# The key-value products of a chunk, made one chunk ahead in the scan's two PSUM banks

## The chip, the cores and the metric

The kernel runs on one core of one Trainium2 chip. Its engines each take their instructions in a fixed order: TensorE (PE; its weight loads, PEld, overlap the matmuls), VectorE (DVE), ScalarE (ACT), GpSimd (POOL), and SyncE (SP), which issues the DMAs. The metric is the device time of one execution in microseconds (us), the median of several runs.

## The reference, cut to what matters

Inputs are q, k, v and a complex decay for 4 batches, 8 heads, 768 time steps and 48 features. In float32:

```python
# a_re, a_im: decay, scaled to a magnitude of at most 0.999
for t in range(768):                               # state S: 48 x 48, complex
    S_re, S_im = ar*S_re - ai*S_im + k[t] v[t]^T,  ar*S_im + ai*S_re
    y[t] = q[t] @ S_re
# x = y, heads side by side: (4, 768, 384)
u  = x + real(fft(fft(x, over time), over features))
un = (u - mean) / sqrt(var + 1e-6)                 # over the 384 features
u  = u + relu(un @ w_ch1) @ w_ch2                  # 384 -> 1536 -> 384
u  = u + (relu(u^T @ w_tok1) @ w_tok2)^T           # tokens: 768 -> 256 -> 768
out = u + relu(u @ w_ch1b) @ w_ch2b                # 384 -> 1536 -> 384
```

## The kernel before

The work of a batch is a chain and a dense part. **The chain** (`chain`) begins with `stage1`: a scan along time over the decays, which uses the two PSUM banks of tag "p", then a test that sets a gate (`st_g2`), then the recurrence in 8 chunks of 96 time steps. Behind it comes `stage2`, in which the Fourier sums are made on VectorE (L988, L994, L1005) and TensorE (L1028, L1039, L1044, L1086), and the normalization (L1091 to L1120; ScalarE's last step is L1118). `transposed` (L899 to L911) then turns the normalized tiles: TensorE L906, ScalarE L909 (th, the high part), VectorE L910 (tl, the low part). **The dense part** is `mlp` (TensorE L926 and L948; VectorE adds into u at L951), `tok1` (L1153) and `tok2` (L1171; VectorE L1173). Every fp32 matrix product there is three products of high and low parts. `mlp` takes three token tiles of 128 at once in L926, so it begins when the third of them has its th and tl.

While the chain of batch b+1 runs, the dense part of batch b fills TensorE (in the driver: `chain(b + 1)`, then `dense1(b)` and `mlp2`). The order on each engine is fixed when the program is built, by a scheduler that takes the ready instruction of the best priority: on TensorE the chain goes ahead of the dense work, on the other engines the dense work ahead of the chain (`RANK`, L60). In batch 0 there is no dense work to fill in; there the weights are converted to high and low parts (L185 to L207: VectorE L194 and L199, GpSimd L196 and L206, ScalarE L191 and L205), and stored. Later batches load the converted weights (L283).

**A chunk c.** `ch_load` (L739) issues from SP the DMA of V (L741, tag "P", 2 buffers) and two of Kn, the scaled keys (L744, tag "A", 2 buffers). `ch_sc` (L748) makes the scores, TensorE L753, masked by VectorE (L760). `ch_u` (L763) makes the key-value products (L768 and L769, 8 heads, 16 matmuls), and the state's step from them: VectorE adds the products to the state T (Aa, L779) and multiplies by the decay (Xx, L785), VectorE or GpSimd makes the crossed part (yc, L786 and L787), VectorE adds to the new T (L789). `ch_y` (L794) makes the outputs, scores times V (L802) and state times queries (L808), which ScalarE copies out to xT (L810).

PSUM has eight banks: three of tag "s" (scores, and in batches 1 to 3 key-value products and outputs too: `PU`), three of tag "l" (dense work, and in batch 0 key-value products and outputs), two of "p". Tiles of a tag take its banks in turn, and a matmul into a bank waits for the last reader of what was there.

Of the kernel before, what the change touches and what calls it, by code (L numbers as in the profile page):

```python
# [53 lines left out]
def attn_fft_mixer_kernel(ctx: ExitStack, tc: tile.TileContext, aL, xL, vL, wL, qN, kN, vN, arN, aiN,  # L54
# [37 lines left out]
    def alloc(tag, shape, dt=F32, name=None):  # L92
        n = 1
        for x in shape[1:]:
            n *= x
        t = pool.tile([128, SIZE[tag]], dt, tag=tag, bufs=BUFS[tag], name=name or tag)
        return shaped(t[0:shape[0], 0:n], shape)
# [3 lines left out]
    def palloc(tag, shape):  # L101
        n = 1
        for s in shape[1:]:
            n *= s
        t = psum.tile([128, 512], F32, tag=tag, bufs=PSB[tag], name=tag)
        v = t[0:shape[0], 0:n]
        if len(shape) == 3:
            v = v.rearrange("p (a b) -> p a b", b=shape[2])
        return v
# [195 lines left out]
    def warm(n, x):  # L305

        ps = palloc("l", [128, 512])
        for _ in range(n):
            te.matmul(out=ps[:, 0:x.shape[1]], lhsT=ident[0:x.shape[0], :], rhs=x)
# [391 lines left out]
    def stage1(b):  # L701
# [34 lines left out]
        st = {}  # L736
        PU = "l" if b == 0 else "s"

        def ch_load(c):  # L739
            v = alloc("P", [96, 384], name="V")  # L740
            sp.dma_start(out=v, in_=vL[b, c])  # L741
            kt = alloc("A", [96, 8, 128], name="Kn")
            for hf in range(2):
                sp.dma_start(out=kt[48 * hf:48 * hf + 48],  # L744
                             in_=knd[hf].rearrange("(h c) s f -> c s h f", c=8)[c])
            st[c] = dict(v=v, kt=kt)

        def ch_sc(c, half):  # L748
            ps = palloc("s", [96, 4, 96])
            Q, K = qk[0][:, 1], qk[0][:, 0]  # L750
            for j in range(4):
                hc = (half * 4 + j) * 8 + c
                te.matmul(out=ps[:, j, :], lhsT=K[:, hc, :], rhs=Q[:, hc, :])  # L753
            sc = alloc("e", [96, 4, 96], name="sc")
            mb = mask.unsqueeze(1).to_broadcast([96, 4, 96])
            if half and OFF[2] & (1 << b):
                se.copy(out=sc, in_=ps)
                ge.tensor_tensor(out=sc, in0=sc, in1=mb, op=ALU.mult)
            else:
                ve.tensor_tensor(out=sc, in0=ps, in1=mb, op=ALU.mult)  # L760
            st[c][f"sc{half}"] = sc

        def ch_u(c):  # L763
            d = st[c]
            ps = palloc(PU, [112, 8, 48])
            for h in range(8):
                vv = d["v"][:, h * 48:h * 48 + 48]
                te.matmul(out=ps[0:64, h, :], lhsT=d["kt"][:, h, 0:64], rhs=vv)  # L768
                te.matmul(out=ps[64:112, h, :], lhsT=d["kt"][:, h, 64:112], rhs=vv)  # L769
            g = gm[b % 2].rearrange("p k (h c) -> p k h c", c=8)[:, :, :, c:c + 1]  # L770

            def gb(k, lo, hi):
                return g[lo:hi, k].to_broadcast([hi - lo, 8, 48])

            def v8(ap):
                return ap.rearrange("p (h e) -> p h e", e=48)
            if c:
                a = alloc("e", [112, 384], name="Aa")
                ve.tensor_tensor(out=v8(a), in0=v8(st["T"]), in1=ps, op=ALU.add)  # L779
                a = v8(a)  # L780
            else:
                a = ps
            y = yc[c % 2]
            x = alloc("e", [112, 384], name="Xx")
            ve.tensor_tensor(out=v8(x), in0=a, in1=gb(0, 0, 112), op=ALU.mult)  # L785
            (ge if c and b else ve).tensor_tensor(out=v8(y)[0:48], in0=a[64:112], in1=gb(1, 64, 112), op=ALU.mult)  # L786
            st["yop"] = (ge if c else ve).tensor_tensor(out=v8(y)[64:112], in0=a[0:48], in1=gb(1, 0, 48), op=ALU.mult)  # L787
            T = alloc("e", [112, 384], name="T")
            st["op"] = ve.tensor_tensor(out=T, in0=x, in1=y, op=ALU.add)  # L789
            st["Tn"] = T  # L790
            if b == 0:
                tops.append(st["op"])
# [23 lines left out]
        ch_load(1)  # L816
        ch_sc(0, 0)
        ch_sc(0, 1)
        for c in range(8):
            if c < 7:  # L820
                ch_u(c)
                ch_sc(c + 1, 0)
                ch_sc(c + 1, 1)
            ch_y(c)
            if b == 0 and WC[c]:
                warm(WC[c], ident)
            st["T"] = st.get("Tn")
            if c < 6:
                ch_load(c + 2)
            if b == 0 and c < 7:  # L830
                rests[0], rests[1] = tops[c], st["yop"]
                tick(CF[c + 1], c == 5)
# [368 lines left out]
    def on(s, f, *args):  # L1201
        stream[0] = s
        return f(*args)

    def chain(b):
        stage1(b)
        return stage2(b)
# [3 lines left out]
    u, norm = on(FIRST, chain, 0)  # L1211
    t1 = on(FIRST, transposed, u, norm, "s")
    feed(56)
    for b in range(B - 2):
# [8 lines left out]
        u = u1  # L1223
# [12 lines left out]
    with tc.If(fv != 0):  # L1236
        with tc.For_i(0, B, 1) as b:
            fallback(b)
            u, norm = stage2(B)
# [113 lines left out]
```

## Time and profile before

| | us |
|---|---|
| median of 3 runs | 1102.06 (1101.85 to 1102.67) |
| profiled execution, span of the trace | 1097.6 |
| what lies outside the span (median less span) | 4.5 |
| TensorE busy in the span | 981.1 (89%) |
| VectorE busy | 776.3 (71%) |
| ScalarE busy | 511.7 (47%) |
| GpSimd busy | 420.9 (38%) |

The profiled execution is known by its span; the times of the runs hold a start and an end besides. The chunks of the four batches stand at about 84 to 143, 350 to 405, 545 to 584 and 732 to 782 us of the span. In the rows, an operation has the tile that it writes, "<-", the tiles that it reads, and "x" the number of such instructions in the row. A matmul of fp32 data has two records in the trace for one in the program's order. In square brackets stands how long the engine was idle before, and whose instruction ended that. "SPq" is the queue of DMA issues.

### The profile page before, as it was taken

To read this page: it belongs to the slowest core of one execution; us is meant where nothing else is said; L and a number is where in the kernel's file an instruction comes from. 1 tells how busy PE (TensorE), PEld (TensorE's weight loads), DVE (VectorE), ACT (ScalarE), POOL (GpSimd) and SP (SyncE) were. 2 spreads that over 40 slices of the span, in tenths; PEclk is the share of its full clock that TensorE was granted. 3 is DMA by queue.
4 is the path that set the end of the run, shared out by engine and by line. 5 is a ranking of instruction groups with operands and counts; after the bars stand their busy time and mean duration, and the time that the engine had idled before them with its cause. 6 is when DMAs were issued, how large, how long until landed. Compare 5 with 4: busy or idle time off the path is not lost.

```text
span 1097.6 us, 21079 instructions
## 1 busy us (share of the span) xinstructions
PE 981.1 (89%) x7314; PEld 919.2 (84%) x7314; DVE 776.3 (71%) x2083; ACT 511.7 (47%) x1425; POOL 420.9 (38%) x552
## 2 busy tenths in 40 slices
PE   1358797999889989799998999999897999999997
PEld 0227675989889887799997899999786999999997
DVE  6986987999999668999758879984744433433332
ACT  6753355777877225968315556842234212121111
POOL 6643985573576454345336312424512002000000
PEclk9997797999999999799999999999998999999999
DMA  6136954686758663356664346664303433443432
GB/s 217 45 82 180 298 175 152 220 272 196 233 182 274 201 185 124 110 165 180 158 192 147 107 138 194 186 184 131 122 29 115 144 116 130 159 154 127 165 101 75
DMA packets 101537, 174.66 MB, mean 159 GB/s; under 512 B 11056, under 2 KB 61104, under 8 KB 100912
## 3 DMA queue, kind: packets, MB, share of 16 engines
q1 hardware_dynamic: 101424, 173.24, 51.1%
q8 instruction: 60, 0.98, 0.4%
q14 instruction: 53, 0.43, 0.1%
HBM read 133.88 MB, written 39.32 MB: 158 GB/s over the span
## 4 chain that ended last, share of the span: by engine, by line
PE 64%; DVE 10%; ACT 2%; DMA 2%; issue 1%; POOL 1%; SPq 0%; POOLq 0%; DVEq 0%; ACTq 0%
PE l L948 23%; PE l L926 21%; PE s L753 3%; PE s L642 2%; PE s L1039 2%; PE s L802 2%; DVE ws L994 2%; PE s L1028 1%; PE s L808 1%; PE s L1153 1%; PE s L768 1%; DVE ws L988 1%; PE s L1171 1%; DVE cvt L199 1%; PE s L906 1%
## 5 line engine op out<-in xcount | busy, mean ns | idle before, releaser
L948 PE MATMUL l<-w,h 128*128 128x384 f32 x1728 | 326.8, 340 | 5.7 <-DVE h L939 5.1
L926 PE MATMUL l<-th,w 128*128 128x384 f32 x1152 | 317.2, 344 | 8.8 <-DVE u L951 5.0
L948 PEld LDWEIGHTS l<-w,h 128*128 128x128 f32 x1728 | 298.4, 189 | 10.0 <-DVE h L939 7.2
L926 PEld LDWEIGHTS l<-th,w 128*128 128x128 f32 x1152 | 212.9, 191 | 13.3 <-DVE u L951 6.3
L926 PE MATMUL l<-tl,w 128*128 128x384 f32 x576 | 196.0, 340 | 3.6 <-DVE tl L910 3.6
L930 ACT ACTIVATE h<-l 128x384 fp32r<-128x384 f32 x192 | 94.0, 490 | 212.7 <-PE l L926 212.0
L951 DVE TENSOR_TENSOR u<-u,l 128x384 f32<-128x384 f32 x192 | 105.3, 549 | 81.9 <-PE l L948 80.9
L939 DVE SCALAR_TENSOR_TENSOR h<-l,h 128x384 fp32r<-128x384 f32 x160 | 88.4, 553 | 88.5 <-ACT h L930 88.3
L926 PEld LDWEIGHTS l<-tl,w 128*128 128x128 f32 x576 | 110.1, 191 | 4.1 <-DVE tl L910 4.1
L196 POOL TENSOR_TENSOR cvt<-cvt 128x384 int32<-128x384 int32 x56 | 64.7, 1160 | 36.7 <-DVE cvt L194 11.0
L466 PE MATMUL s<-misc,y 128*112 128x128 f32 x96 | 21.7, 369 | 53.1 <-DVE y L444 48.8
L466 PEld LDWEIGHTS s<-misc,y 128*112 128x112 f32 x96 | 14.0, 177 | 62.3 <-issue 26.8
L753 PE MATMUL s<-qkt 112*96 112x96 f32 x512 | 59.2, 266 | 6.7 <-DVE sc L760 6.7
L753 PEld LDWEIGHTS s<-qkt 112*96 112x96 f32 x512 | 53.2, 177 | 9.4 <-DVE sc L760 7.4
L1138 POOL TENSOR_TENSOR xl<-u,xh 128x384 fp32r<-128x384 f32 x18 | 17.9, 1006 | 105.6 <-ACT xh L1137 105.6
L206 POOL TENSOR_TENSOR w<-cvt,w 128x384 fp32r<-128x384 f32 x44 | 51.2, 1172 | 9.9 <-ACT w L205 6.1
L199 DVE SCALAR_TENSOR_TENSOR cvt<-cvt 128x384 int32<-128x384 int32 x56 | 48.1, 865 | 7.0 <-POOL cvt L196 6.8
L571 POOL TENSOR_TENSOR tm<-tm 128x144 f32<-128x144 f32 (+1 forms) x51 | 27.1, 531 | 59.0 <-ACT tm L570 58.7
L937 POOL TENSOR_TENSOR h<-full,h 128x384 fp32r<-128x384 f32 x32 | 33.6, 1049 | 35.5 <-ACT full L936 33.7
L642 PE MATMUL s<-misc,y 128*112 128x128 f32 x288 | 45.0, 276 | 1.4 <-DVE y L626 1.0
L615 DVE TENSOR_TENSOR p<-p,A 128x144 f32<-128x144 f32 x144 | 44.6, 310 | 2.2
L786 POOL TENSOR_TENSOR yc<-Aa,gm 48x384 f32<-48x384 f32 x18 | 21.0, 1164 | 63.3 <-DVE Aa L779 63.3
(234 smaller groups left out, 1950.8 us busy)
## 6 DMA issues: line engine op xcount, KB each, us to landing
w<-wscr SPq DMA_DIRECT2D x180, 384.0 KB, 3.5
cvt<-wL SPq DMA_DIRECT2D x56, 384.0 KB, 4.6
wscr<-w SPq DMA_DIRECT2D x44, 384.0 KB, 3.5
Kn<-kn SPq DMA_DIRECT2D x64, 192.0 KB, 3.7
kn<-y SPq DMA_DIRECT2D x96, 96.0 KB, 2.5
raw<-aL SPq DMA_DIRECT2D x48, 144.0 KB, 3.2
xx<-xL SPq DMA_DIRECT2D x48, 144.0 KB, 3.1
V<-vL SPq DMA_DIRECT2D x32, 144.0 KB, 3.1
```

What stands on the lines that cost most here:

```text
L196: x = ge.tensor_tensor(out=a, in0=a, in1=lo, op=ALU.add)
L199: rest(ve.scalar_tensor_tensor(out=a, in0=hi, scalar=-0x80000000, in1=a, op0=ALU.bitwise_and, op1=ALU.bitwise_or))
L206: ge.tensor_tensor(out=parts[:, 1, :], in0=a.bitcast(F32), in1=r32(parts[:, 0, :]), op=ALU.subtract)
L466: te.transpose(ps[:, j, :], y[:, j, 0:112], ident)
L615: ve.tensor_tensor(out=cur, in0=prev, in1=A[:, j, 0:3, :], op=ALU.mult)
L642: te.transpose(ps[:, j, :], y[:, j, 0:112], ident)
L753: te.matmul(out=ps[:, j, :], lhsT=K[:, hc, :], rhs=Q[:, hc, :])
L926: te.matmul(out=ps, lhsT=w1[:, wi, kt * 128:kt * 128 + 128], rhs=x[g][:, kt, :], start=(n == 0), stop=(n == 8))
L930: x = se.activation(out=hi, in_=ps, func=ACTF.Relu)
L939: ve.scalar_tensor_tensor(out=lo, in0=ps, scalar=0.0, in1=r32(hi), op0=ALU.max, op1=ALU.subtract)
L948: te.matmul(out=ps, lhsT=hs[m][:, hi, tt * 128:tt * 128 + 128], rhs=w2[:, wi, :], start=(n == 0), stop=(n == 8))
L951: ve.tensor_tensor(out=u[tt], in0=u[tt], in1=ps, op=ALU.add)
```

## The change

`ch_u` is split. `ch_m(c)` makes the 16 key-value products, and into a "p" bank; `ch_u(c)` only reads them. `ch_m(0)` is called before the loop, `ch_m(c + 1)` at the start of step c for c below 6. The scores and outputs stay on their banks.

```diff
-        def ch_u(c):
+        def ch_m(c):
+
             d = st[c]
-            ps = palloc(PU, [112, 8, 48])
+            ps = d["u"] = palloc("p", [112, 8, 48])
             for h in range(8):
                 vv = d["v"][:, h * 48:h * 48 + 48]
                 te.matmul(out=ps[0:64, h, :], lhsT=d["kt"][:, h, 0:64], rhs=vv)
                 te.matmul(out=ps[64:112, h, :], lhsT=d["kt"][:, h, 64:112], rhs=vv)
+
+        def ch_u(c):
+            ps = st[c]["u"]
...
         ch_sc(0, 1)
+        ch_m(0)
         for c in range(8):
             if c < 7:
+                if c < 6:
+                    ch_m(c + 1)
                 ch_u(c)
                 ch_sc(c + 1, 0)
                 ch_sc(c + 1, 1)
```

In the changed kernel the lines shift: the key-value products are L769 and L770, the outputs L806 and L812, and lines behind the chunk loop are 7 higher (L906 becomes L913, L926 L933, L948 L955, L988 L995, L1028 L1035, L1171 L1178, L1173 L1180). The order of the dense work around the chain moves with them.

The first place is TensorE in the chunks of batch 1. L768 and L769 (L769 and L770 after) are the key-value products, L753 the scores, L948 (L955) dense work, L802 and L808 (L806 and L812) the outputs. Before:

```order
686 L768 MATMUL s<-V,Kn 64x48
687 L769 MATMUL s<-V,Kn 48x48
688 L753 MATMUL s<-qkt 96x96 x8
689 L948 MATMUL l<-w,h 128x384 x11
690 L802 MATMUL s<-sc,V 64x96
691 L802 MATMUL s<-sc,V 48x96
692 L808 MATMUL s<-qkt,T 64x96
693 L808 MATMUL s<-qkt,T 48x96
```

After:

```order
718 L955 MATMUL l<-w,h 128x384 x11
719 L806 MATMUL s<-sc,V 64x96
720 L806 MATMUL s<-sc,V 48x96
721 L812 MATMUL s<-qkt,T 64x96
722 L812 MATMUL s<-qkt,T 48x96
723 L806 MATMUL s<-sc,V 64x96
724 L769 MATMUL p<-V,Kn 64x48
725 L770 MATMUL p<-V,Kn 48x48
...
740 L806 MATMUL s<-sc,V 48x96
741 L812 MATMUL s<-qkt,T 64x96
...
750 L812 MATMUL s<-qkt,T 48x96
751 L753 MATMUL s<-qkt 96x96 x8
```

The key-value products, before between the outputs of one chunk and the scores of the next, stand inside the outputs, and write "p" instead of "s".

The second place is TensorE behind the last outputs of batch 2's chunks. L1178 is the second token-mixing product (L1171 before), L906 (L913) the transposes of the tiles u of the dense work, L926 (L933) the first dense product behind them, L1028 (L1035) the first product of the mixing. Before:

```order
1427 L808 MATMUL s<-qkt,T 48x96
1428 L906 MATMUL l<-misc,u_3218 128x128 x3
1429 L926 MATMUL l<-th,w 128x384
1430 L926 MATMUL l<-tl,w 128x384
...
1453 L926 MATMUL l<-th,w 128x384
1454 L1028 MATMUL s<-dcos,ws 128x97 x5
```

After:

```order
1402 L812 MATMUL s<-qkt,T 48x96
1403 L1178 MATMUL l<-R,w 128x384 x19
1404 L913 MATMUL l<-misc,u_3213 128x128 x3
1405 L913 MATMUL l<-misc,u_3214 128x128 x3
1406 L913 MATMUL l<-misc,u_3215 128x128 x3
1407 L913 MATMUL l<-misc,u_3216 128x128 x3
1408 L1035 MATMUL s<-dcos,ws 128x97 x3
1409 L913 MATMUL l<-misc,u_3217 128x128 x3
1410 L1035 MATMUL s<-dcos,ws 128x97 x9
1411 L913 MATMUL l<-misc,u_3218 128x128 x3
1412 L933 MATMUL l<-th,w 128x384
```

Before, dense products (36 in all, in pieces of one or two) stood between the last transposes and the first mixing products; after, the end of the token mixing and six groups of transposes stand there, and dense products begin behind the second piece of the mixing.

On VectorE at the same place, L1173 (L1180) adds the token mixing into u, L910 (L917) makes tl, and L988, L994 and L1005 (L995, L1001 and L1012) are the first steps of the mixing. Before:

```order
1297 L760 TENSOR_TENSOR sc<-s,misc 96x384 x2
1298 L910 TENSOR_TENSOR tl<-l,th 128x3x128 x3
1299 L988 TENSOR_TENSOR ws<-xT 112x4x288
1300 L988 TENSOR_TENSOR ws<-xT 112x4x96
1301 L994 TENSOR_TENSOR ws<-ws 112x2x288
1302 L910 TENSOR_TENSOR tl<-l,th 128x3x128
1303 L994 TENSOR_TENSOR ws<-ws 112x2x288
1304 L994 TENSOR_TENSOR ws<-ws 112x2x96 x2
...
1306 L994 TENSOR_TENSOR ws<-ws 112x2x288
1307 L1005 TENSOR_TENSOR ws<-ws 112x2x191 x2
```

After:

```order
1292 L995 TENSOR_TENSOR ws<-xT 112x4x288
1293 L1180 TENSOR_TENSOR u_3215<-u_3215,l 128x384
1294 L995 TENSOR_TENSOR ws<-xT 112x4x96
1295 L1180 TENSOR_TENSOR u_3216<-u_3216,l 128x384
1296 L1001 TENSOR_TENSOR ws<-ws 112x2x288 x2
1297 L1180 TENSOR_TENSOR u_3217<-u_3217,l 128x384
1298 L1001 TENSOR_TENSOR ws<-ws 112x2x96 x2
...
1300 L1180 TENSOR_TENSOR u_3218<-u_3218,l 128x384
1301 L917 TENSOR_TENSOR tl<-l,th 128x3x128
1302 L1001 TENSOR_TENSOR ws<-ws 112x2x96
1303 L1012 TENSOR_TENSOR ws<-ws 112x2x191 x4
...
1308 L917 TENSOR_TENSOR tl<-l,th 128x3x128
```

The tl of the first token tiles, before made ahead of or inside the mixing's first steps, stand behind most of them.

The third place is TensorE at the end of batch 3's chain, where L906 (L913) turns the normalized tiles and L1153 (L1160) is the first token-mixing product of batch 2. Before:

```order
2096 L1086 MATMUL s<-misc,xT 128x112 x4
2097 L1086 MATMUL s<-misc,ws 128x112 x4
2098 L948 MATMUL l<-w,h 128x384 x9
2099 L906 MATMUL s<-misc,ws 128x128 x18
2100 L1153 MATMUL s<-xh,w 128x384 x10
```

After:

```order
2072 L955 MATMUL l<-w,h 128x384 x6
2073 L913 MATMUL s<-misc,ws 128x128 x6
2074 L955 MATMUL l<-w,h 128x384 x2
2075 L913 MATMUL s<-misc,ws 128x128 x3
2076 L955 MATMUL l<-w,h 128x384 x19
2077 L913 MATMUL s<-misc,ws 128x128 x3
2078 L955 MATMUL l<-w,h 128x384 x8
2079 L913 MATMUL s<-misc,ws 128x128 x3
2080 L955 MATMUL l<-w,h 128x384 x19
2081 L1160 MATMUL s<-xh,w 128x384 x5
```

The 18 transposes stood together behind the last dense products that were left; after, dense products stand among and behind them.

## Rows read from the trace of the kernel before

**Rows 1.** Stretches: window, length, busy PE, PEld, DVE, ACT, POOL, clock, DMA, GB/s

```profile
84.00:143.00 59.00, 47.69 (x640) 44.12 (x636) 47.49 (x86) 20.74 (x45) 40.94 (x31) 0.77 0.84 252
...
350.00:405.00 55.00, 53.56 (x724) 50.31 (x723) 35.48 (x79) 16.27 (x36) 22.72 (x22) 1.00 0.71 196
405.00:450.00 45.00, 34.56 (x200) 28.20 (x199) 40.29 (x123) 26.75 (x84) 21.99 (x32) 0.84 0.40 128
...
545.00:584.00 39.00, 39.00 (x603) 35.95 (x602) 22.46 (x44) 7.87 (x16) 12.44 (x13) 1.00 0.62 179
584.00:600.00 16.00, 11.43 (x60) 10.78 (x58) 16.00 (x21) 8.43 (x27) 13.26 (x11) 0.89 0.56 170
...
782.00:837.00 55.00, 44.51 (x266) 38.96 (x264) 33.72 (x69) 20.37 (x55) 23.54 (x22) 0.92 0.25 84
```

**Rows 2.** TensorE's timeline, a chunk and dense work: start, us, operation, idle before

```profile
372.38 0.34 PE L808 MATMUL s<-qkt,T 112*48 112x96 f32 x4
...
373.57 0.92 PE L753 MATMUL s<-qkt 112*96 112x96 f32 x8
...
377.09 0.38 PE L802 MATMUL s<-sc,V 96*64 96x96 f32 x4
...
378.30 0.34 PE L808 MATMUL s<-qkt,T 112*48 112x96 f32 x4
...
463.69 6.50 PE L948 MATMUL l<-w,h 128*128 128x384 f32 x36
```

**Rows 3.** VectorE by line: busy, mean ns, idle before and its releaser

```profile
L779 DVE TENSOR_TENSOR Aa<-T,s 112x384 f32<-112x384 f32 x18 | 10.0, 554 | 24.6 <-PE s L769 24.6
```

**Rows 4.** Weight loads by line

```profile
L802 PEld LDWEIGHTS s<-sc,V 96*48 96x48 f32 (+1 forms) x384 | 20.4, 129 | 5.3 <-DVE T L789 3.0 <-issue 2.3
```

**Rows 5.** SP's timeline in the same chunk of batch 1

```profile
372.60 0.33 SPq L741 DMA_DIRECT2D V<-vL  x1
373.69 1.07 SPq L744 DMA_DIRECT2D Kn<-kn  x2
```

**Rows 6.** Landing of V (L741), batch 1, 355 to 400

```profile
DMA to landing us min/median/max: 2.2/2.8/4.3
```

**Rows 7.** Landing of Kn (L744), batch 1, 355 to 400

```profile
DMA to landing us min/median/max: 2.9/3.4/5.3
```

**Rows 8.** VectorE's timeline in batch 0's chunks

```profile
96.61 0.56 DVE L779 TENSOR_TENSOR Aa<-T,l 112x384 f32<-112x384 f32 x1 [0.72 <-PE l L769]
...
121.64 0.56 DVE L789 TENSOR_TENSOR T<-Xx,yc 112x384 f32<-112x384 f32 x1 [1.81 <-POOL yc L787]
```

**Rows 9.** TensorE's timeline behind batch 1's chunks

```profile
421.08 2.73 PE L1028 MATMUL s<-dcos,ws 112*128 112x97 f32 x24
...
442.31 1.54 PE L906 MATMUL s<-misc,ws 128*128 128x128 f32 x6 [4.38 <-ACT ws L1118]
445.65 1.54 PE L906 MATMUL s<-misc,ws 128*128 128x128 f32 x6 [1.80 <-ACT ws L1118]
```

**Rows 10.** TensorE's timeline behind batch 2's chunks

```profile
583.31 0.55 PE L906 MATMUL l<-misc,u 128*128 128x128 f32 x3
...
589.18 0.45 PE L926 MATMUL l<-tl,w 128*128 128x384 f32 x1 [3.57 <-DVE tl L910]
...
597.42 0.46 PE L1028 MATMUL s<-dcos,ws 112*128 112x97 f32 x2 [1.00 <-DVE ws L1005]
```

**Rows 11.** VectorE by line, 583 to 600

```profile
L994 DVE TENSOR_TENSOR ws<-ws 112x576 f32<-112x576 f32 (+1 forms) x6 | 5.3, 902 | 0.0
L1005 DVE TENSOR_TENSOR ws<-ws 112x382 f32<-112x382 f32 x6 | 4.9, 862 | 0.0
L988 DVE TENSOR_TENSOR ws<-xT 112x1152 f32<-112x1152 f32 (+1 forms) x2 | 4.3, 2172 | 0.2 <-PE s L808 0.2
```

**Rows 12.** TensorE's timeline behind batch 3's chunks

```profile
793.03 0.44 PE L926 MATMUL l<-th,w 128*128 128x384 f32 x1 [3.17 <-DVE u L951]
...
835.73 1.54 PE L906 MATMUL s<-misc,ws 128*128 128x128 f32 x6 [6.33 <-ACT ws L1118]
```

## The prediction, made before the result was known

> **What bounds the kernel now.** I read first the table of stretches [rows 1]. In the chunk phases of batches 1 to 3 TensorE is busy without a break: 53.56 of 55 us from 350 to 405, 39.00 of 39 from 545 to 584. The idle time that counts lies elsewhere: in batch 0's chunks (84 to 143, 47.69 of 59 us busy) and in the three boundaries behind the chunks of batches 1 to 3, where the mixing and the normalization of the batch run: 405 to 450 (34.56 busy, 10.4 idle), 584 to 600 (11.43 busy, 4.6 idle), 782 to 837 (44.51 busy, 10.5 idle). I call them B1, B2 and B3. TensorE's amount of work does not change, so I count only how its idle time changes.
>
> I use these short names: M for the 16 key-value products of a chunk, SC for its scores, Y for its outputs, D for one dense matmul of 384 columns (36 take 6.50 us, 0.18 us each [rows 2]).
>
> Second, TensorE's timeline of one chunk [rows 2]: the end of Y comes every 5.92 us (372.38 and 378.30), and between lie M (about 1.0 us, up to 373.57), SC, 11 D and Y. Third, who waits there. VectorE's addition Aa waits for M in all: 24.6 us before 18 instructions [rows 3], over 1 us a chunk. It looks like the very thing to remove, but TensorE has no gap there; its loads of weights for Y wait 3.0 us in all for T [rows 4].
>
> **The change part by part.** The same 16 matmuls are made, into the two "p" banks, which are idle once the scan is over. Nothing is added on VectorE, GpSimd or ScalarE. What moves is order.
>
> *Chunk phases, batches 1 to 3.* VectorE's 24.6 us of waits go, but each chunk still has 11 D between SC and Y in the new order. A TensorE that was full stays full, so the 24.6 us are worth nothing directly; the most to be had is the 3.0 us for T, and I take −1 (0 to −3).
>
> Against this stands a new dependence. The load of V for chunk c+2 waits for Y(c), because V has two buffers. M(c+2) now stands inside Y(c+1), a whole step earlier. From the end of Y(c) to it TensorE has SC (16 matmuls, 8 take 0.92, so at most 1.8), 11 D (2.0) and the first 5 of Y's 32 matmuls (about 0.25, as Y takes 1.4 us between 377.09 and 378.5) [rows 2]: 4.0 us. Before, V was wanted a chunk later. V is issued as Y ends (372.60) and the two Kn pieces 1.1 us behind it [rows 5]. V's landing takes 2.2/2.8/4.3 us (least, median, most) [rows 6]; so at the median it is in time by 1.2 us, at the worst 0.3 late. Now the two Kn go ahead of V, since M(c+1), which frees their buffer, ends before Y(c) does. A Kn takes 2.9/3.4/5.3 us [rows 7]. The two issues take 1.07 us [rows 5] and begin about 1 us before Y's end, the second so some 0.4 us ahead of V's. If V lands with it, that is 3.0 at the median (in time) and 4.9 at the worst (0.9 late). A late V stops TensorE, with Y's remainder and all D queued behind M, and then VectorE, so it is pure loss. There are 15 such places (V of chunks 2 to 6, three batches). Bounds 0 and 15 × 0.9 = 13; the median rows are nearest to the low end, and I take a fifth of the places at 0.7: +2.
>
> The Trainium skill (DMA: Bandwidth & Descriptors, Queues, rings and completion order) says that descriptors on one ring are taken in the order of issue, which speaks against the change: V's bytes go behind Kn's. By it V lands no earlier than Kn's last bytes, the case just bounded by 4.9 us; by V's own row alone the term would be near 0. No row of before shows V directly behind two Kn in a steady chunk.
>
> *Batch 0's chunks.* Here VectorE and GpSimd also convert weights, in a fixed order. Aa waited for M once, 0.72 us; T waited up to 1.81 us for GpSimd's yc [rows 8], which the move does not make earlier. I take −0.4; −2 to +3, by one or two such waits more or fewer.
>
> *The boundaries.* The scheduler redistributes the D of the batch before. Counted along TensorE's order, the D done by the end of the last Y are 876 before and 866 now in batch 1, 1440 and 1421 in batch 2, 2180 and 2107 in batch 3. What is not spent inside the chunks is left as cover for the boundary.
>
> B1: 10 more D are left. TensorE waited 4.38 and 1.80 us for ScalarE's normalized tiles after its D had run out [rows 9]. 10 × 0.18 = 1.8 fill part of it: −2 (0 to −4).
>
> B2: the gap was 3.57 us for VectorE's tl and 1.00 for its ws [rows 10], and 36 D stood ahead of the first mixing products. Now 19 of the second token-mixing layer and six transposes come first, and the next D need the third tl, which VectorE makes behind its first work on the mixing: 2 L988 (4.3), 6 L994 (5.3), 6 L1005 (4.9) [rows 11], four additions L1173 and three tl at 0.55 each (3.9; 0.55 as Aa's mean [rows 3]) and one small one (0.3): 18.7, and since neighbours overlap by a twentieth, 17.8 us from the last Y. In them TensorE has 19 D (3.4), 18 transposes (3 take 0.55 [rows 10]: 3.0 at most) and 24 passes of L1028 (2.73 [rows 9]): 9.1. So 8.7 us are idle where 4.6 were: +4.1. If VectorE's additions fall into its waits it is +1; if transposes and products overlap wholly, +8.
>
> B3: the D ran out before the transposes of the batch's end, and TensorE waited 6.33 us for ScalarE's last tiles [rows 12] and 0.6 in two short waits. Now 48 D stand among and right behind these transposes, and 29 of them (5.2 us) before the last. This covers most of the 6.9 us. In front 43 D instead of 52 stand ahead of the first mixing product, so the front gap, 3.17 us for VectorE's u [rows 12], grows by 9 × 0.18 = 1.6. I take 5.2 + 1.4 (the D ahead of the first transpose are 131 instead of 124) − 1.6 = 5.0: −5 (0, if the normalization moves back as far as the D reach; −8, if all goes and the front does not grow).
>
> Sum: −1 + 2 − 0.4 − 2 + 4.1 − 5 = −2.3 us on a span of 1097.6. The median of the runs, 1102.06, lies 4.5 us above the span, for what is outside it; I add it unchanged: 1097.6 − 2.3 + 4.5 = 1099.8, and round to 1100.
>
> **The rivals.** A: V's load takes the place of the wait removed. Place: M inside Y, 15 times; price up to 0.9 us each; it decides once V lands more than 4.0 us after Y's end. For it speaks the order on SP's queue, against it the medians 2.8 and 3.4. With 0.7 us at every place: 15 × 0.7 = 10.5 in place of 2, so 1100 + 8.5 = 1108, slower.
>
> B: the cover of the boundaries is worth more than I count: B3 gives its 8, B1 its 4, B2 loses 1, chunks +0.5: −1 + 0.5 − 0.4 − 4 + 1 − 8 = −12, so 1090; at half the way 1095. For it speaks that 73 D fewer are spent before the last Y of batch 3.
>
> C: B2 opens wholly (+8), and B3 gives 0 because the chain that ends there moves back with it: −1 + 2 − 0.4 − 2 + 8 = +6.6, so 1109, slower. For it speaks that the transposes for the next dense layer now stand behind the mixing on VectorE.
>
> E: the waits of VectorE were on the path after all. The Trainium skill (Perfetto Trace Analysis, Identifying Performance Opportunities) says that the same gap repeated on the engine that should be saturated can mean too little PSUM for the next tile. Here the repeated gap, about 1.1 us a chunk, stands on VectorE, and TensorE has none [rows 1]. If it did count, all 24.6 us would go: 1102 − 25 = 1077.
>
> That the change does nothing is the case in which the boundaries cancel: 1102.
>
> **How the numbers follow.** The measurement tells 0.2% from no change, about 2.2 us: the bounds are 1099.9 and 1104.3. My forecast lies at the edge of them, since it is a difference of terms of about 4 each. Chances: the forecast case, with terms near those taken (1097 to 1103), 0.41; A 0.14; B 0.25; C 0.14; E 0.03; no effect beyond that 0.03. Half of the forecast case lies below 1099.9 (0.18) and the rest in the band. So faster 0.18 + 0.25 + 0.03 = 0.46 and same 0.23 + 0.03 = 0.26, slower 0.28. Range: from the middle of B, 1092, to C's end, 1109; the forecast case's own range is 1097 to 1103.
>
> **What would show it.** Right: Aa waits for M no longer, TensorE still full and a chunk still near 5.9 us; V's landing under 4 us and no wait for a DMA in front of M; TensorE idle near 9 us behind batch 2's last Y, ended by tl; B3's last wait for ScalarE near 1 us. Wrong: chunks shorter than 5.9 us (E), waits for V in front of M (A), B2 as short as before (B), or the 6.33 us still there (C).

## The result, and the profile after

The changed kernel takes 1115.08 us (median of 4 runs, 1114.49 to 1115.32) against 1102.09 for the kernel before in the same series: a ratio of 1.0116, 95% interval 1.0102 to 1.0130. It is slower by 13 us, outside the range of 1092 to 1109.

The spans are 1097.6 and 1112.7 us. Every run whose span is on record is 1.7 to 2.3 us longer than it, so the execution behind the trace of before took some 1099.4 us: of the 4.5 us that the table of before gives as outside the span, some 2.7 are only that this execution was faster than the median, and so are some 2 of the 15 us between the two traces. To see where the 15 us went I cut both traces at the same events (first scores of a batch, last outputs, last transposes of the normalized tiles), and take off what the moved dense products explain, at 0.175 us each (three in a row take 0.52). "D" is the number of dense products of 384 columns in a stretch. The last column is the time that is lost, or with a minus sign won.

| stretch | us before | us after | D before | D after | lost |
|---|---|---|---|---|---|
| start to first scores of batch 1 | 354.4 | 357.5 | 780 | 774 | +4.1 |
| batch 1, scores to last outputs | 49.2 | 56.0 | 97 | 93 | +7.5 |
| B1, to the last transposes | 45.7 | 48.8 | 59 | 70 | +1.2 |
| to first scores of batch 2 | 86.4 | 87.3 | 420 | 417 | +1.4 |
| batch 2, scores to last outputs | 47.7 | 42.6 | 84 | 68 | −2.4 |
| B2 and the rest of its mixing, to the last transposes | 58.7 | 62.5 | 180 | 153 | +8.5 |
| to first scores of batch 3 | 93.5 | 92.6 | 472 | 467 | −0.1 |
| batch 3, scores to last outputs | 45.9 | 42.5 | 89 | 66 | +0.6 |
| B3, to the last transposes | 55.8 | 59.3 | 124 | 178 | −5.9 |
| rest, to TensorE's last product | 254.5 | 257.0 | 1439 | 1458 | −0.8 |

(15 transposes, 2.6 us, moved from batch 2's chunks into B2: so these two rows are +0.2 and +5.9 of real loss. Behind TensorE's last product 0.9 us more pass after than before.)

Here are stretches of the trace after, cut at these events, to be set beside [rows 1]: the chunks of batch 0, chunks and boundary of batch 1, chunks of batch 2, B2 up to its first L1035 and then up to the first transposes of the normalized tiles, chunks and boundary of batch 3. The columns are those of [rows 1].

```profile
84.00:143.30 59.30, 46.04 (x638) 42.42 (x634) 48.10 (x85) 21.36 (x47) 37.38 (x30) 0.78 0.81 235
357.20:413.30 56.10, 50.73 (x688) 47.01 (x686) 32.77 (x69) 12.25 (x24) 19.23 (x19) 0.94 0.58 159
413.30:462.10 48.80, 37.43 (x219) 30.98 (x213) 42.52 (x124) 30.45 (x92) 23.53 (x33) 0.85 0.42 131
549.30:591.90 42.60, 42.46 (x653) 39.45 (x653) 23.59 (x50) 6.08 (x11) 14.41 (x14) 1.00 0.60 165
591.90:606.10 14.20, 6.37 (x37) 5.05 (x33) 13.84 (x16) 7.08 (x17) 12.75 (x10) 0.83 0.73 246
606.10:641.30 35.20, 34.94 (x201) 31.07 (x202) 29.08 (x104) 22.43 (x78) 11.95 (x25) 0.88 0.26 75
746.90:789.50 42.60, 42.09 (x660) 39.40 (x658) 24.33 (x53) 6.03 (x12) 13.93 (x14) 1.00 0.53 129
789.50:848.80 59.30, 55.41 (x327) 49.99 (x322) 34.86 (x73) 23.07 (x58) 22.40 (x21) 0.94 0.22 71
```

Batches 2 and 3 are full in their chunks, as before. Batch 1's chunks are not: 5.4 us of idle time and a granted clock of 0.94.

A steady chunk on TensorE in batch 2, to be set beside [rows 2] (start, us, operation):

```profile
574.10 0.33 PE L812 MATMUL s<-qkt,T 112*48 112x96 f32 x3
574.36 1.60 PE L753 MATMUL s<-qkt 112*96 112x96 f32 x16
...
577.83 0.38 PE L806 MATMUL s<-sc,V 96*64 96x96 f32 x4
...
579.98 0.33 PE L812 MATMUL s<-qkt,T 112*48 112x96 f32 x3
```

From outputs to outputs it is 5.88 us (574.10 to 579.98), as the 5.92 before. VectorE and the weight loads, to be set beside [rows 3, 4]; the first row is VectorE's, the second of the weight loads:

```profile
L783 DVE TENSOR_TENSOR Aa<-T,p 112x384 f32<-112x384 f32 x24 | 13.2, 549 | 17.9 <-PE p L770 17.9
```

```profile
L806 PEld LDWEIGHTS s<-sc,V 96*48 96x48 f32 (+1 forms) x384 | 23.4, 132 | 4.4 <-issue 3.9
```

Aa's wait fell from 24.6 us before 18 instructions to 17.9 before 24, and it is still the products that Aa waits for. The wait for T (3.0 us) is gone. Neither shows in the chunk's time.

In batch 1's chunks the products wait for V and Kn. SP's timeline and then TensorE's (start, us, operation, idle before), and the windows around the first wait (columns as in [rows 1]):

```profile
367.87 0.32 SPq L207 DMA_DIRECT2D wscr<-w  x1
368.32 2.92 SPq L744 DMA_DIRECT2D Kn<-kn  x4
371.35 0.40 SPq L741 DMA_DIRECT2D V<-vL  x1
...
387.50 0.96 SPq L744 DMA_DIRECT2D Kn<-kn  x2
388.55 0.56 SPq L741 DMA_DIRECT2D V<-vL  x1
```

```profile
375.51 0.23 PE L769 MATMUL p<-V,Kn 96*64 96x48 f32 x1 [1.99 <-DMA V<-vL]
...
393.74 0.23 PE L769 MATMUL p<-V,Kn 96*64 96x48 f32 x1 [1.49 <-DMA V<-vL]
```

```profile
369.00:375.00 6.00, 4.52 (x35) 4.24 (x29) 4.75 (x10) 0.58 (x1) 1.99 (x2) 1.00 0.87 202
375.00:381.00 6.00, 5.49 (x71) 5.04 (x71) 2.13 (x5) 0.00 (x0) 1.52 (x2) 0.58 0.30 68
381.00:387.00 6.00, 6.00 (x79) 5.75 (x79) 2.26 (x5) 1.09 (x2) 1.51 (x2) 0.85 0.09 25
```

The first outputs of the batch end at 369.2. V could be issued then, but SP is busy with four Kn until 371.24, behind a store of converted weights (L207) that had waited 5.1 us for GpSimd's conversion (L206). SP's waits for it in batch 1's chunks, first before (357 to 405 us) and then after (the same window):

```profile
SPq L207 <- POOL w L206: 3.7, 3, 2.0
```

```profile
SPq L207 <- POOL w L206: 13.6, 4, 5.9
```

V lands 4.0 us after its issue, and the products begin 6.3 us after the outputs; TensorE waits 1.99. At the second place V was issued 0.8 us after the outputs, behind two Kn, and took 5.1 us to land, the longest of the batch. There are also two waits for Kn in front of the products of chunks 0 and 1, 1.2 us in all, for which the prediction had no term.

Behind the first wait the granted clock is 0.58 on average for 6 us, near the lower of its two levels (1.2 of 2.4 GHz), and 0.85 for the next 6. An estimate from these rows is 0.42 × 5.5 + 0.15 × 6 = 3.2 us more, which is more than the wait itself. Behind the second wait (1.49 us) the clock stayed at 1.00:

```profile
393.00:399.00 6.00, 5.26 (x77) 4.92 (x79) 2.41 (x5) 1.07 (x2) 2.00 (x2) 1.00 0.59 159
```

V's landing in the chunks of batches 1, 2 and 3 after, one row each:

```profile
DMA to landing us min/median/max: 2.1/3.6/5.1
```

```profile
DMA to landing us min/median/max: 2.2/3.3/3.9
```

```profile
DMA to landing us min/median/max: 2.3/3.4/4.0
```

In batches 2 and 3 V stays within the 4.0 us that the prediction gave it, and the chunks have 0.5 us of waits in all; in batch 1 it does not. The median rose from 2.8 in batch 1 [rows 6] to 3.6, with Kn in front of most of them. The last V of batch 2 and that of batch 3, with no Kn directly in front, landed in 2.2 and 2.3 us; the rule of the Trainium skill (DMA: Bandwidth & Descriptors, Queues, rings and completion order) that descriptors on a ring are taken in order agrees with that.

B2 on TensorE, to be set beside [rows 10]:

```profile
592.06 3.57 PE L1178 MATMUL l<-R,w 128*128 128x384 f32 x19
597.07 0.55 PE L913 MATMUL l<-misc,u 128*128 128x128 f32 x3 [1.44 <-DVE u L1180]
599.95 0.55 PE L913 MATMUL l<-misc,u 128*128 128x128 f32 x3 [2.33 <-DVE u L1180]
603.04 1.54 PE L913 MATMUL l<-misc,u 128*128 128x128 f32 x6 [2.55 <-DVE u L1180]
606.36 1.60 PE L1035 MATMUL s<-dcos,ws 112*128 112x97 f32 x6 [1.77 <-ACT ws L1019]
```

The four waits are 8.1 us. The clock is 0.83 in the stretch that holds most of them and 0.88 in the 35 us behind it; before, it was 0.89 [rows 1] and then 1.00:

```profile
600.00:642.00 42.00, 42.00 (x266) 38.11 (x265) 33.41 (x119) 25.51 (x79) 11.34 (x24) 1.00 0.35 101
```

In B1 the largest wait, to be set beside [rows 9], and in B3 the waits and transposes that answer to [rows 12]:

```profile
455.23 1.54 PE L913 MATMUL s<-misc,ws 128*128 128x128 f32 x6 [5.89 <-ACT ws L1125]
```

```profile
801.48 2.98 PE L1035 MATMUL s<-dcos,ws 112*128 112x97 f32 x14 [2.73 <-ACT ws L1019]
...
842.11 0.82 PE L913 MATMUL s<-misc,ws 128*128 128x128 f32 x6
843.12 0.49 PE L913 MATMUL s<-misc,ws 128*128 128x128 f32 x3
846.78 0.49 PE L913 MATMUL s<-misc,ws 128*128 128x128 f32 x3
```

The transposes at batch 3's end no longer wait: the 6.33 us are gone.

### The profile page after: what moved, and what is told of

Same layout as the page of the kernel before. It is cut to its first block, busy times and chain, and to the rows that moved or that the text cites. A ratio compares the mean times of both kernels' runs of the same rounds, so it can differ in the third digit from the quotient of the medians.

```text
span 1112.7 us, 21032 instructions
## 1 busy us (share of the span) xinstructions
PE 991.8 (89%) x7314; PEld 924.9 (83%) x7314; DVE 778.1 (70%) x2083; ACT 513.9 (46%) x1425; POOL 419.4 (38%) x552
## 4 chain that ended last, share of the span: by engine, by line
PE 47%; DVE 3%; DMA 1%; ACT 0%; issue 0%; DVEq 0%; SPq 0%
PE l L955 17%; PE l L933 16%; PE s L753 2%; PE s L1035 1%; PE s L1046 1%; PE s L806 1%; PE s L1178 1%; PE s L1160 1%; DVE ws L1001 1%; PE s L642 1%; PE s L812 1%; PE p L769 1%; DVE ws L995 1%; PE s L913 1%; PE l L1160 1%; PE s L1093 1%
## 5 line engine op out<-in xcount | busy, mean ns | idle before, releaser
L955 PE MATMUL l<-w,h 128*128 128x384 f32 x1728 | 328.1, 342 | 7.9 <-DVE h L946 5.5
L933 PE MATMUL l<-th,w 128*128 128x384 f32 x1152 | 315.6, 343 | 4.8 <-DVE u L958 2.0
L955 PEld LDWEIGHTS l<-w,h 128*128 128x128 f32 x1728 | 300.8, 190 | 12.6 <-DVE h L946 7.6
L933 PEld LDWEIGHTS l<-th,w 128*128 128x128 f32 x1152 | 211.2, 190 | 9.4 <-DVE h L946 3.7
L933 PE MATMUL l<-tl,w 128*128 128x384 f32 x576 | 195.2, 339 | 0.0
L958 DVE TENSOR_TENSOR u<-u,l 128x384 f32<-128x384 f32 x192 | 105.4, 549 | 84.3 <-PE l L955 83.8
L933 PEld LDWEIGHTS l<-tl,w 128*128 128x128 f32 x576 | 109.4, 190 | 1.0 <-issue 0.5
L753 PE MATMUL s<-qkt 112*96 112x96 f32 x512 | 58.1, 268 | 9.6 <-DVE sc L760 9.6
L753 PEld LDWEIGHTS s<-qkt 112*96 112x96 f32 x512 | 51.9, 179 | 13.7 <-issue 6.2
L814 ACT ACTIVATE xT<-s,gate 112x384 f32<-112x384 f32 x24 | 13.9, 580 | 93.8 <-PE s L812 76.7
L206 POOL TENSOR_TENSOR w<-cvt,w 128x384 fp32r<-128x384 f32 x44 | 48.3, 1102 | 12.7 <-ACT w L205 6.8
L589 POOL TENSOR_TENSOR A<-raw,tm 128x144 f32<-128x144 f32 (+1 forms) x51 | 26.4, 519 | 58.1 <-DVE yt L616 28.9
```

The source lines that it names most:

```text
L206: ge.tensor_tensor(out=parts[:, 1, :], in0=a.bitcast(F32), in1=r32(parts[:, 0, :]), op=ALU.subtract)
L933: te.matmul(out=ps, lhsT=w1[:, wi, kt * 128:kt * 128 + 128], rhs=x[g][:, kt, :], start=(n == 0), stop=(n == 8))
L955: te.matmul(out=ps, lhsT=hs[m][:, hi, tt * 128:tt * 128 + 128], rhs=w2[:, wi, :], start=(n == 0), stop=(n == 8))
L958: ve.tensor_tensor(out=u[tt], in0=u[tt], in1=ps, op=ALU.add)
```

## The experiments

Each kernel was timed beside the kernel before; the ratios are to it, with 95% intervals. Losses in a stretch are cut as in the table, from one trace each. In the kernels that keep the old place of the products in some batch, lines behind the chunk loop stand 10 higher than before (L906 is L916, L926 L936, L948 L958, L951 L961, L1028 L1038, L1118 L1128, L1153 L1163, L1173 L1183).

**The change in one batch at a time.** The edit, for batch 0, against the changed kernel:

```diff
-            ps = d["u"] = palloc("p", [112, 8, 48])
+            ps = d["u"] = palloc("p" if b in (0,) else PU, [112, 8, 48])
...
         def ch_u(c):
+            if b not in (0,):
+                ch_m(c)
...
-        ch_m(0)
+        if b in (0,):
+            ch_m(0)
...
-                if c < 6:
+                if c < 6 and b in (0,):
```

> The change in batch 0 alone (products ahead and in the p banks there, batches 1 to 3 as before). Theory A (the loss of the whole change is made of separate pieces: late Kn and V in batch 1, dense work moved out of batch 2's boundary, a slower clock behind batch 0's chunks, and a gain at batch 3's end): the chunks of batch 0 stay within 1 us, and up to 4 us are lost behind them, so 1102 to 1106. Theory B (the moved products slow every chunk, in every batch by a similar 3 to 4 us): 1105 to 1106, with the 3 to 4 us between the first scores and the last outputs of batch 0.

Measured: 1.0083 (1.0059 to 1.0107), some 9 us slower. Up to the first scores of batch 1 5.1 us are lost, but only 1.7 of them in batch 0's chunks. Another 5.9 are lost in batch 3's chunks and B3: 2218 dense products were done before its last outputs instead of 2180, so that they ran out even earlier. Neither theory foresaw that second part, and the time lies outside what both gave.

For batch 1 (the tuples of the same four places):

```diff
-            if b not in (0,):
+            if b not in (1,):
```

> The change in batch 1 alone. Theory A: 7 to 8 us are lost in batch 1's chunks, by waits for the DMAs of Kn and V in front of the products and by the lower clock behind these waits; with a few us either way in later batches, whose dense work moves, 1106 to 1112. Theory B: 3 to 4 us lost, 1105 to 1106.

Measured: 1.0098 (1.0075 to 1.0121). 4.5 us are lost in batch 1's chunks, less than theory A's 7 to 8, with two waits for V (the row: engine, tile, line, what it waited for, us, times, longest):

```profile
PE p L769 <- DMA V<-vL: 2.9, 2, 1.7
```

Behind the longer of them the clock was 0.72 for 6 us. Another 6.6 us are lost from batch 3's last outputs on, again by dense work that runs out earlier (2209 done at the last outputs).

For batch 2:

```diff
-            if b not in (1,):
+            if b not in (2,):
```

> The change in batch 2 alone; up to batch 2's chunks the order is that of before. Theory A: the chunks keep their time, the boundary behind them loses about 6 us (TensorE idle about 8 us instead of 4.6 behind the last outputs, for VectorE's additions into u, and a lower clock then), and the 53 dense products that are left over give some 4 back at batch 3's end, where the 6.3 us wait shrinks: 1102 to 1105. Theory B: 3 to 4 us lost in the chunks of batch 2: 1105 to 1106.

Measured: 1.0006 (0.9988 to 1.0024). As theory A has it, the waits of B2 are there (row below), 6.0 us are lost there after the transposes that moved, and 7.4 come back in B3. The chunks lose 1.6 us with these transposes counted, which theory A did not have: one V took 5.1 us to land there, and the products waited 1.4 us for a load.

```profile
PE l L916 <- DVE u L1183: 6.3, 3, 2.6
```

For batch 3:

```diff
-            if b not in (2,):
+            if b not in (3,):
```

> The change in batch 3 alone; all before batch 3's chunks is as before. Theory A: the chunks keep their time (within 1 us), the 36 dense products left over fill the 6.3 us wait at the batch's end: 1097, 5 us faster than before. Theory B: 3 to 4 us lost in the chunks, part of the gain at the end kept: 1100 to 1106.

Measured: 0.9935 (0.9914 to 0.9956), 7 us faster. The waits behind batch 3's chunks, first before and then with the edit:

```profile
PE s L906 <- ACT ws L1118: 6.3, 1, 6.3
PE l L926 <- DVE u L951: 3.6, 2, 3.2
```

```profile
PE l L958 <- DVE u L961: 4.0, 2, 3.2
PE s L916 <- ACT ws L1128: 0.6, 1, 0.6
```

The 6.3 us have gone to 0.6, and the chunks lost nothing. Theory B, a toll on every chunk, is out: four batches show four different amounts, from 4.5 us down to none.

**A third buffer for V in batch 1.** Against the kernel with the change in batch 1 alone:

```diff
-            v = alloc("P", [96, 384], name="V")
+            v = alloc("f" if b in (1,) and c % 3 == 2 else "P", [96, 384], name="V")
```

> The change in batch 1 alone, as in the earlier run of that name, but every third V of batch 1 goes to a third buffer (one that the dense part of batch 0 does not use), so that V of chunk c+2 waits for the outputs of chunk c-1 and not of c. Theory A (the loss in batch 1's chunks is the late V): no wait for V in front of the products; the order now has almost no dense work between the chunks, and 44 more dense products are left for the boundary behind them, whose 10 us of idle time shrink to 4 to 6: 1095 to 1100, faster than before by 3 to 7. Theory C (the weights' stores and loads on SP's queue ahead of Kn and V, and the traffic they make, are what delays; the buffers are not): waits for Kn or V stay, 3 us or more lost in the chunks: 1104 to 1112.

Measured: 1.0017 (1.0002 to 1.0032). The waits in batch 1's chunks and the 11 us behind them (the first row is behind):

```profile
PE l L936 <- DVE u L961: 2.3, 1, 2.3
PE s L753 <- DVE sc L760: 2.1, 2, 1.1
```

No wait for V is left, and the chunks lose 0.8 instead of 4.5 us: the cause of that piece is shown, and theory C, by which the buffers are not the cause, is out. The time expected was wrong. The 61 dense products more than before that are left for B1 lengthen it by all that they take; its idle time stays 9.5 us (10.4 before). None of them stands among the batch's last transposes, where TensorE still waits 4.8 us.

**The bank without the look-ahead.** In batch 1, and in batch 3. The edits are written as against the kernel before; in the source of these runs `ch_m` stays and is called first in `ch_u`, which makes the products at their old place:

```diff
-            ps = palloc(PU, [112, 8, 48])
+            ps = palloc("p" if b in (1,) else PU, [112, 8, 48])
```

> Half of the change, in batch 1 alone: the products go to the p banks, but stand where they stood before (behind the outputs of the chunk before). Theory A: no DMA comes late, as nothing is wanted earlier; the order has no or few dense products inside a chunk, so TensorE waits for the state some 1.5 us in each of five chunks, 7 us, and the 48 dense products that are left over give that back in the boundary behind: 1099 to 1106. Theory D (the p banks alone cost time): a loss above 8 us in the chunks, 1107 or more.

Measured: 1.0010 (0.9993 to 1.0027). No product of batch 1 waits for a DMA, and the chunks lose 1.0 us.

```diff
-            ps = palloc("p" if b in (1,) else PU, [112, 8, 48])
+            ps = palloc("p" if b in (3,) else PU, [112, 8, 48])
```

> The same half in batch 3 alone. Theory A (the gain of the change in batch 3 is the dense products that are left for the batch's end, not the earlier products): the 6.3 us wait at the end goes as it did with the look-ahead, and five chunks lose about 1.5 us each to the wait for the state, partly given back by the 31 dense products more: 1095 to 1101. Theory E (the gain comes from the look-ahead itself): no faster than before, 1102 or more.

Measured: 0.9938 (0.9922 to 0.9955), the same as with the look-ahead in batch 3 (0.9935). The bank alone gives the gain. In this kernel's batch 3 few dense products stand in the chunks; two of the scores, with the window over six chunks:

```profile
753.27 1.52 PE L753 MATMUL s<-qkt 112*96 112x96 f32 x16
...
757.12 1.60 PE L753 MATMUL s<-qkt 112*96 112x96 f32 x16
```

```profile
736.00:773.00 37.00, 35.74 (x606) 33.84 (x604) 20.91 (x43) 6.35 (x13) 14.01 (x14) 1.00 0.52 132
```

A chunk takes 3.9 us without dense work, and TensorE is still busy 97%: the expected 1.5 us of waiting in each chunk are not there, since products, scores and outputs alone nearly fill it; with so short a chunk one V came 1.3 us late even without the look-ahead. The 65 dense products not spent there (2115 against 2180 at the last outputs) are the cover of B3.

**Batch 1 with the third buffer and batch 3.** Against the kernel with the change in batch 3 alone (the tuples of the four places):

```diff
-            if b not in (3,):
+            if b not in (1, 3):
...
-            v = alloc("P", [96, 384], name="V")
+            v = alloc("f" if b in (1,) and c % 3 == 2 else "P", [96, 384], name="V")
```

> Batch 1 with the look-ahead and the third buffer for V, and batch 3 with the plain look-ahead. Theory A: both gains add up, as the batches between keep the order of before: 1088 to 1094. Theory C: the loss in batch 1 takes the gain of batch 3: 1097 to 1104.

Measured: 0.9950 (0.9932 to 0.9969), near the sum of what 1.0017 and 0.9935 gave alone, and between the two expectations. The batch 3 gain stands, batch 1 adds none.

**The bank alone in all batches.**

```diff
-            ps = palloc(PU, [112, 8, 48])
+            ps = palloc("p", [112, 8, 48])
```

> Half of the change in all batches: the products in the p banks, but where they stood before, behind the outputs of the chunk before. Theory A (nothing comes late without the look-ahead; what counts is which dense work is left for the boundaries): no wait for V in front of the products; behind batch 2's chunks now stand 28 products of the first and 18 of the second token mixing, 8 us of work, so that the idle time there is 3 to 6 us, not over 8; the wait at batch 3's end is gone. 1093 to 1099, faster than before by 3 to 9. Theory F (the p banks for batches 0 to 2 cost what the whole change cost there): 1108 or more.

Measured: 0.9950 (0.9936 to 0.9964), faster by 5.5 us, as theory A has it. The look-ahead, with the order of the dense work that it brings, makes the difference between 0.9950 and 1.0116.

**The third buffer in batch 2 alone.** Against the kernel with the change in batch 2 alone:

```diff
-            v = alloc("P", [96, 384], name="V")
+            v = alloc("tmp" if b in (2,) and c % 3 == 2 else "P", [96, 384], name="V")
```

> The change in batch 2 alone, with a third buffer for every third V. Theory A: behind the last outputs now stand 3 dense products and 36 of the first token mixing instead of 19 of the second and its transposes, so the idle time there falls from 8 to 3 to 6 us, and batch 3's end keeps its 50 products: 1096 to 1101. Theory G (the chain's own work behind batch 2, VectorE's first, sets that hole whatever stands there): 8 us idle as in the run without the third buffer, 1101 to 1104.

Measured: 0.9980 (0.9964 to 0.9996). In B2 the first token mixing now stands behind the last outputs, and the waits are these:

```profile
PE s L1038 <- ACT ws L1022: 3.0, 1, 3.0
PE l L1163 <- POOL xl L1148: 1.9, 1, 1.9
```

4.9 us instead of 8.1: what dense work stands there decides, not VectorE's mixing alone. Against the run without the third buffer the time is hardly apart (0.9980 and 1.0006, and the intervals overlap a little).

**The whole change with the third buffer.** Against the changed kernel:

```diff
-            v = alloc("P", [96, 384], name="V")
+            v = alloc("f" if b in (0, 1) and c % 3 == 2 else "tmp" if b in (2, 3) and c % 3 == 2 else "P", [96, 384], name="V")
```

> The whole change, with a third buffer for every third V in every batch. Theory A: no wait for V in front of the products in batches 1 to 3, the 4 to 7 us of batch 1's chunks come back, and with the boundary of batch 2 as in the run of batch 2 alone: 1096 to 1104, some 11 to 19 faster than the change as it is. Theory C (the look-ahead loses time in other ways): 1108 to 1115.

Measured: 0.9995 (0.9977 to 1.0014). The 13 us come back with one more buffer for V. That the order of the dense work moves with it is part of this gain, and how large a part was not tried. The profiled execution is the longest of the ten (1106.75 against the median of 1100.97): 12 us are lost in it before batch 1's first scores, most of them behind batch 0's chunks. From one trace it can't be told whether that is this execution's or the buffer's in batch 0.

**The bank in batch 0 alone.**

```diff
-            ps = palloc(PU, [112, 8, 48])
+            ps = palloc("p" if b in (0,) else PU, [112, 8, 48])
```

> The products in the p banks in batch 0 alone, at their old place. The dense work keeps its order. Theory A (in batch 0 the order of the conversions is all that counts, and the look-ahead moved it): same as before, 1100 to 1104. Theory F (the p banks cost time in batch 0): 1106 or more, as in the run with the look-ahead in batch 0 alone.

Measured: 1.0001 (0.9987 to 1.0016): nothing.

**How the loss divides.** Three more kernels. First, the changed kernel with the look-ahead taken back in batch 0:

```diff
+            if b not in (1, 2, 3):
+                ch_m(c)
...
-        ch_m(0)
+        if b in (1, 2, 3):
+            ch_m(0)
...
-                if c < 6:
+                if c < 6 and b in (1, 2, 3):
```

> The changed kernel with the look-ahead taken back in batch 0 alone (its products stay in the p banks, which alone cost nothing). Theory A (batch 0's look-ahead holds 3 to 5 us of the whole change's loss): 1109 to 1112. Theory H (the loss seen in and behind batch 0 is the spread that this stretch shows in any run, and batch 0's look-ahead costs only by the phase in which it puts the dense work later): 1113 to 1116 here, since the order of the later boundaries is that of the changed kernel.

Measured: 1.0088 (1.0059 to 1.0116), about 3 us less than the whole change; the intervals overlap, and neither theory is decided. Its trace reaches batch 1's first scores at 358.2 us, no earlier than the changed kernel (357.5), so the loss of that stretch is there without the look-ahead too. Its waits in batch 1's chunks are these, and the window behind the longer wait for V shows no fall of the clock:

```profile
PE p L769 <- DMA V<-vL: 2.6, 2, 1.4
PE p L769 <- DMA Kn<-kn: 0.9, 2, 0.6
```

```profile
372.80:378.80 6.00, 6.00 (x92) 5.74 (x93) 3.73 (x8) 0.58 (x1) 2.62 (x3) 1.00 0.43 93
```

These chunks lose 2.7 us, against 7.5 in the changed kernel's trace. Second, the changed kernel with the third buffer in batch 1 alone:

```diff
-            v = alloc("P", [96, 384], name="V")
+            v = alloc("f" if b in (1,) and c % 3 == 2 else "P", [96, 384], name="V")
```

> The changed kernel with the third buffer for V in batch 1 alone. Theory A (the late V of batch 1 is the largest single piece, 7 us): no wait for V in batch 1's chunks, 1106 to 1110; the boundary of batch 2 keeps its hole of 8 us and batch 3 its gain. Theory H (V's wait in batch 1 was a part of it only): 1111 to 1115.

Measured: 1.0066 (1.0040 to 1.0093), 5.5 us less than the change. In batch 1's chunks nothing is lost (−0.1 instead of +7.5). Third, batches 1 to 3 with the third buffer, batch 0 as before (against the kernel with the change in batch 0 alone; the tuples of the four places):

```diff
-            if b not in (0,):
+            if b not in (1, 2, 3):
...
-            v = alloc("P", [96, 384], name="V")
+            v = alloc("f" if b in (1,) and c % 3 == 2 else "tmp" if b in (2, 3) and c % 3 == 2 else "P", [96, 384], name="V")
```

> Look-ahead in batches 1 to 3 with the third buffer for V there, batch 0 as before. Theory A: no late V, boundary of batch 2 with the first token mixing in front, gain at batch 3's end, batch 0 undisturbed: 1093 to 1098, faster than all batches with the third buffer (1101). Theory H (batch 0 costs nothing by itself): 1099 to 1102, as with all batches.

Measured: 1.0026 (1.0009 to 1.0044), outside what either theory gave. In its trace the stretch from batch 2's last outputs to the transposes is the worst of all (+10 us by the table's measure, 2.6 of them transposes), with 6.4 us of waits where the run with the third buffer in batch 2 alone has 4.9. The chunks of batches 1 to 3 have no wait for V. So time is lost where nothing is late; that it is the phase in which the dense work meets the boundary is likely, and not shown.

## Why the prediction was wrong

The forecast was a small gain, and the time fell outside the range. The sum of the terms was −2.3 us and the traces differ by +15.1. Of the 17 us between, 7.3 lie in the chunks of batches 1 to 3 (+1 taken, +8.3 found), 4.5 in batch 0 and behind it, 3.2 in B1, 1.8 in B2, −0.9 in B3, and 1.4 in stretches that had no term. Step by step:

- *The chunks stay at 11 D, and VectorE's wait for the products is worth nothing.* Right: 5.88 against 5.92 us, though Aa still waits for the products, which the signs had otherwise. The rule on consistent gaps (Trainium skill, Perfetto Trace Analysis, Identifying Performance Opportunities) speaks of the engine that should be saturated; the gap here stood on another, and rival E was rightly small.
- *Late V, +2 (0 to 13).* The step that failed. The mechanism was named and the term was too small: in batch 1's chunks alone 7.5 us are lost. Its limit of 4.0 us after the outputs holds in batches 2 and 3 (574.43 to 578.38 in the steady chunk), where V lands in 3.3 and 3.4 at the median, and next to nothing is lost. Two things were left out of the term. V's issue was taken to follow the outputs at once, yet SP still had four Kn to issue behind a store that waited. And a wait on a full TensorE was priced at its length, while in this trace the clock after it cost more than the wait; that part differs from trace to trace: with waits of 1.4 and 1.7 us the same chunks lost 2.7 and 4.5 us in other kernels. (The first Kn are late too, for which there was no term, but with the third buffer 1.3 us of waits for Kn stay and nothing is lost.) The third buffer takes the piece away (−0.1 instead of 7.5 in the changed kernel, and 0.8 instead of 4.5 with the change in batch 1 alone); of the time it gives back 5.5 of the 13 us, so late V in batch 1 is the largest piece and not the whole. That the queue on SP is what made V late in batch 1 and not in 2 and 3 is read from the trace and was not tried by itself.
- *B2, +4.1 us of idle time.* Right in place and mechanism, 8.1 us of waits where 8.7 were worked out. (Six groups of transposes at 0.55 are 3.3 us and not 3.0, so the sum gives 8.4.) It left out the lower clock in and behind them: the real loss is 5.9.
- *B3, −5.* Right: −5.9 in the whole change, and alone in batch 3 it is a gain of 7. But it was credited to the look-ahead's order, where the bank alone is enough.
- *B1, −2.* Wrong in sign, +1.2: dense work that is left over need not stand in the gap. With 61 products more (the run with the third buffer in batch 1) the idle time of B1 fell by only 0.9 us.
- *Batch 0, −0.4.* The first 357 us lost 4.1. Traces of kernels with batch 0 untouched reach batch 1's first scores at 354.1 to 357.7 us, and the trace of before, at 354.4, is one of the early ones. Taking the look-ahead out of batch 0 brought 3 us with overlapping intervals, and the bank alone changed nothing. Most of this row may be the choice of the trace; how much is batch 0's own stays open.

Two slips of the working change little. The 5 outputs that stand ahead of the products are 5 of 16 in the program's order, not of 32, so 0.44 us and not 0.25; the scores take 1.6 us and not 1.8, and the limit of 4.0 came out right by luck. And the 4.5 us added to the span hold some 2.7 of a fast execution; that does no harm to the sum, which is the median less 2.3 either way.

Of the rivals A was nearest, 1108; it had the places evenly spread, while the loss sits in one batch.

## What to carry to other kernels

When work is moved earlier, work out for each of its inputs when that input's buffer comes free and what stands ahead of its load on the issuing queue; look-ahead with an unchanged number of buffers can move the wait to the load. In a kernel whose order is planned at build time, a local change shifts the filler work everywhere behind it; count how much filler is left at each later gap, and where in the gap it stands, before counting the local gain. Try the parts of a change and its batches one by one: here the bank alone in batch 3 is 0.9938 and the whole change 1.0116.

## What the runs showed of the hardware

In batch 1's chunks a wait of 2.0 us on a TensorE that was otherwise full was followed by 6 us at a granted clock of 0.58 and 6 at 0.85, an estimated 3.2 us of extra time. In the same trace a wait of 1.5 us was followed by a clock of 1.00, and in other kernels waits of 1.7 and 1.4 us by 6 us at 0.72 and at 1.00. With the longer holes of B2 the clock was 0.83 and 0.88, where before it was 0.89 and 1.00.

V's landing in the chunks, with Kn in front of most of the loads, took 3.3 to 3.6 us at the median, up to 5.1, against 2.5 to 3.0, up to 4.4, before; the last V's of batches 2 and 3, with no Kn directly in front, took 2.2 and 2.3.
